# Longer modelled DMA hops for the softmax sums in a statically scheduled kernel

## The chip, the cores and the metric

One core of one Trainium2 chip. The metric is device time in microseconds (us) of one execution. "ScalarE" is ACT in the profile, "VectorE" is DVE, "TensorE" is PE (PEld is its weight load), "GpSimd" is POOL and "SyncE" is SP; SPq is the queue from which SyncE issues DMAs.

## The reference, cut to what matters

The kernel computes two independent heads from inputs of 2048 tokens by 640 features and writes them side by side: a linear state-space recurrence (A), and attention with 32 query heads over one shared key and value head of 20 dimensions (B). The change touches only the softmax of B.

```python
def _B_ref(x, wq, wk, wv, wo):
    B, S, D = x.shape            # 1, 2048, 640
    H = 32
    Dh = D // H                  # 20
    q = (x @ wq).reshape(B, S, H, Dh).transpose(0, 2, 1, 3)
    k = x @ wk
    v = x @ wv
    scores = jnp.einsum("bhqd,bkd->bhqk", q, k) * (Dh ** -0.5)
    p = _softmax(scores, axis=-1)
    o = jnp.einsum("bhqk,bkd->bhqd", p, v)
    return o.transpose(0, 2, 1, 3).reshape(B, S, H * Dh) @ wo
```

## The kernel before

The kernel cuts attention into 32 blocks (4 quarters of the queries times 8 groups of 4 heads), each of 64 score tiles of 128 x 512. TensorE computes a tile into PSUM. Either ScalarE takes its exponential (3 or 2 tiles in one instruction, `PR<-SC`), or VectorE and GpSimd take it by an integer approximation in several passes (`DR<-MB` is the first pass, `DR<-DR` the others; SC and MB name PSUM banks, PR and DR the buffers of the results). TensorE then multiplies the result with the values and sums into one PSUM bank per block (PV). Row 20 of each head's 32 rows holds the softmax sum.

When a block is complete, VectorE evicts the bank to one of two buffers `pvsb`. The sums then go out to DRAM and come back spread over 64 partitions; VectorE takes reciprocals; these go out to DRAM and come back broadcast to all rows; VectorE multiplies (the normalisation, `OT<-pvsb,rdB`). That is four DMA hops for each of 31 blocks. The last block takes another way, through TensorE.

```python
            # in pv(), when a block's last product has been planned
            ev = self.dve(lambda e: e.tensor_copy(p.pvsb[:, slot, :], bank.ap), 620, deps=[op], reads=[bank.key],
                          writes=[f"pvsb{slot}"], prio=self.PVEV,
                          gate=lambda: b < 2 or (b - 2 in self.norm_op and self.s.done([self.norm_op[b - 2]])))
            ...
            self.pv_gate = [ev]          # the next block's PV waits for this eviction: one bank
```

No order of instructions is written down by hand. When the kernel is built, a scheduler plays it through with an assumed duration for every operation, picks at each moment the ready operation with the smallest `prio` for each engine, and so fixes every engine's program order. The emitter then puts semaphore waits where data dependencies need them. After that nothing of the assumed times is left, only the order. A DMA's assumed end is:

```python
        if op.dma_key is not None:                       # in Schedule.begin()
            self.free[eng] = self.t + op.tail * len(op.fns)
            s = max(self.t + 1300.0, self.dma_free.get(eng, 0.0))
            self.dma_free[eng] = s + op.dur
            op.end = max(s + op.dur + 700.0, self.free[eng] + 1700.0) + op.land
```

A transposing load is one operation of five DMAs that nothing in the queue can pass. The row of biases `brow` that each query block needs goes into QT by a DMA on the same queue:

```python
        self.ct_op = [self.loadT([(p.CT[:, ri, cd, :], src[:, 128 * cd:128 * cd + 128]) for cd in range(NC)], 819200,
                                 f"ct{ri}", writes=[f"CT{ri}"]) for ri, src in ((0, self.C_re), (1, self.C_im))]
        ...
        self.row_op[(qb, half)] = self.dma(fns, 32768, f"row{rs}", ...   # QT<-brow
```

## Time and profile before

The three runs before the change were 785.99 to 786.46 us, median 786.22 us. The profiled execution has a span of 782.0 us (its time as a run was 783.7 us, so it was faster than those three).

| reading | value |
|---|---|
| ScalarE busy | 754.3 of 782.0 us (96%) |
| exponentials on ScalarE | 737.4 us for 1625 tiles, 0.454 us a tile |
| tiles on VectorE | 423 of 2048 |
| VectorE busy | 654.7 us (84%) |
| VectorE idle before the 31 reciprocals / 31 normalisations | 0.8 / 1.3 us |

From the profile page of the kernel before: the busy time of each engine (share of the span, instructions), and the chain of waits that ended last, by engine.

```profile
PE 731.7 (94%) x10475; PEld 245.0 (31%) x10475; DVE 654.7 (84%) x1193; ACT 754.3 (96%) x675; POOL 444.7 (57%) x460
...
ACT 66%; PE 25%; DVE 5%; DMA 1%; SPq 1%; issue 1%; POOL 0%; ACTq 0%; DVEq 0%; POOLq 0%
```

The Trainium skill, "Perfetto Trace Analysis", section "Identifying the Most-Contended Engine", takes the engine with the highest occupancy as the one to look at; here that is ScalarE (96%), and the chain of waits agrees (66%). From the groups of instructions of the same page: what is written and read, count, then busy us and mean ns of one, then the idle time just before them and who ended most of it.

```profile
L1068 ACT ACTIVATE PR<-SC 128x1536 bf16<-128x1536 f32 (+1 forms) x650 | 737.4, 1340 | 8.6 <-PE MB L571 5.2
...
L586 DVE TENSOR_SCALAR DR<-MB 128x512 int16<-128x512 f32 x423 | 282.7, 684 | 79.2 <-PE MB L571 74.8
```

The count of `DR<-MB`, 423, is the number of tiles that VectorE got. ScalarE's idle time before exponentials is 8.6 us in the whole run. The groups of VectorE in the kernel before, the two that the change is about:

```profile
L581 DVE TENSOR_TENSOR OT<-pvsb,rdB 128x512 bf16<-128x512 bf16 x31 | 16.8, 541 | 1.3 <-DMA rdB<-recs 1.3
...
L1360 DVE RECIPROCAL rc<-dn 64x32 bf16<-64x32 bf16 x31 | 10.4, 334 | 0.8 <-DMA dn<-sums 0.8
```

So VectorE waited for these hops twice in the run, 2.1 us together. Below, VectorE's stream around block 6, from the timeline of the kernel before (start us, duration us, instruction), with all other instructions left out. Evictions at 190.93, 213.82 and 238.63 us are those of blocks 6, 7 and 8.

```profile
190.93 0.69 DVE L1337 CAST pvsb<-MB 128x512 bf16<-128x512 f32 x1
...
196.68 0.33 DVE L1360 RECIPROCAL rc<-dn 64x32 bf16<-64x32 bf16 x1
...
202.94 1.26 DVE L581 TENSOR_TENSOR OT<-pvsb,rdB 128x512 bf16<-128x512 bf16 x1
...
213.82 0.68 DVE L1337 CAST pvsb<-MB 128x512 bf16<-128x512 f32 x1
...
229.04 0.41 DVE L581 TENSOR_TENSOR OT<-pvsb,rdB 128x512 bf16<-128x512 bf16 x1
...
238.63 0.68 DVE L1337 CAST pvsb<-MB 128x512 bf16<-128x512 f32 x1
```

Block 6 is normalised 11 us after the end of its eviction. Its buffer is needed again at 238.63 us, 34 us after the end of the normalisation.

### The profile page before, as it was taken

What the parts mean: (1) busy time and instruction counts of PE and PEld (TensorE: products, weight loads), DVE (VectorE), ACT (ScalarE), POOL (GpSimd) and SP (SyncE); (2) the same over time, 40 slices, a digit from 0 to 9 for tenths busy, and PEclk for the clock granted to TensorE, in tenths of its full rate; (3) what the DMA queues carried; (4) which work ended last, traced back from release to release, by engine and by line L of the source; (5) the groups of instructions that cost most, each with busy time, mean ns of one, the idle gap of its engine ahead of it and who ended that gap; (6) DMA issues with size and microseconds to landing.
All of it is one profiled execution on the core that took longest, in us unless ns stands there. A gap on an engine that the chain in (4) does not pass through costs nothing.

```text
span 782.0 us, 24237 instructions
## 1 busy us (share of the span) xinstructions
PE 731.7 (94%) x10475; PEld 245.0 (31%) x10475; DVE 654.7 (84%) x1193; ACT 754.3 (96%) x675; POOL 444.7 (57%) x460
## 2 busy tenths in 40 slices
PE   8989998998999999989999999989999999999998
PEld 3322222322233333323233223323222322333333
DVE  5989898999988888888989868987789788856995
ACT  5999999999999999999999999999999999999995
POOL 6066566346555556566654754655773456578661
PEclk9999999999999999999999999999999999999999
DMA  9740200000001000020000000110000000010001
GB/s 213 129 78 9 51 9 8 10 3 9 9 10 24 20 18 24 16 43 17 13 12 18 27 16 17 29 29 17 9 16 9 24 23 15 22 30 23 9 9 36
DMA packets 54186, 21.60 MB, mean 28 GB/s; under 512 B 43464, under 2 KB 54080, under 8 KB 54080
## 3 DMA queue, kind: packets, MB, share of 16 engines
q1 hardware_dynamic: 52072, 19.87, 11.7%
q8 instruction: 83, 1.36, 0.7%
q10 hardware_dynamic: 2008, 0.18, 0.2%
q14 instruction: 23, 0.19, 0.1%
HBM read 7.20 MB, written 5.50 MB: 16 GB/s over the span
## 4 chain that ended last, share of the span: by engine, by line
ACT 66%; PE 25%; DVE 5%; DMA 1%; SPq 1%; issue 1%; POOL 0%; ACTq 0%; DVEq 0%; POOLq 0%
ACT PR L1068 66%; PE MB L571 10%; PE MB L567 8%; PE SC L571 7%; DVE DR L586 1%; DMA vrow<-in_A_Dskip_dram 1%; PE SC L567 1%; SPq L556 1%; DVE QT L918 1%; DMA xaT<-in_A_x_dram 0%; DVE VS L585 0%; DVE xbT L797 0%; DVE WO L720 0%; DVE aq L585 0%; DVE fr L586 0%
## 5 line engine op out<-in xcount | busy, mean ns | idle before, releaser
L1068 ACT ACTIVATE PR<-SC 128x1536 bf16<-128x1536 f32 (+1 forms) x650 | 737.4, 1340 | 8.6 <-PE MB L571 5.2
L581 POOL TENSOR_TENSOR DR<-DR,step 128x512 int32<-128x512 int32 x421 | 430.8, 1046 | 315.0 <-DVE DR L586 114.9
L586 DVE TENSOR_SCALAR DR<-MB 128x512 int16<-128x512 f32 x423 | 282.7, 684 | 79.2 <-PE MB L571 74.8
L571 PE MATMUL SC<-QT,KT 32*128 32x512 bf16 x1625 | 253.9, 384 | 35.4 <-ACT PR L1068 25.6
L571 PE MATMUL MB<-DR,VS 128*32 128x512 bf16 x1692 | 225.8, 385 | 2.5 <-DVE pvsb L1337 1.1
L571 PE MATMUL MB<-PR,VP 128*32 128x512 bf16 x1625 | 225.5, 385 | 0.7 <-DVE pvsb L1337 0.3
L571 PE MATMUL MB<-QT,KT 32*128 32x512 bf16 x423 | 154.1, 384 | 2.7 <-DMA QT<-brow 1.8
L571 PEld LDWEIGHTS SC<-QT,KT 32*128 32x128 bf16 x1625 | 64.4, 91 | 268.6 <-ACT PR L1068 178.7
L586 DVE TENSOR_SCALAR DR<-DR 128x1024 int16<-128x1024 int16 (+1 forms) x222 | 83.5, 425 | 7.8 <-PE MB L571 5.6
L571 PEld LDWEIGHTS MB<-PR,VP 128*32 128x32 bf16 x1625 | 57.0, 94 | 66.4 <-issue 49.3
L571 PEld LDWEIGHTS MB<-DR,VS 128*32 128x32 bf16 x1692 | 55.9, 94 | 65.9 <-issue 35.2
L567 PE MATMUL MB<-xaT,BT 128*32 128x512 bf16 x800 | 57.8, 382 | 1.0 <-DMA xaT<-in_A_x_dram 1.0
L581 DVE TENSOR_TENSOR prod<-MB,Z 128x1024 bf16<-128x1024 f32 x40 | 48.7, 1218 | 7.3 <-PE MB L567 6.6
L571 PE MATMUL MB<-xbT,wqf 128*32 128x512 bf16 x640 | 49.0, 387 | 0.7 <-DVE brow L586 0.5
L571 PEld LDWEIGHTS MB<-QT,KT 32*128 32x128 bf16 x423 | 36.3, 91 | 22.0 <-DVE DR L586 10.4
L571 PE MATMUL MB<-KT,VZ 128*32 128x256 bf16 x796 | 41.6, 275 | 0.0
L567 PE MATMUL MB<-WO,OT 128*32 128x128 bf16 (+1 forms) x928 | 40.8, 292 | 0.0
L1633 DVE TENSOR_TENSOR_SCAN g<-sc,hst,u 128x512 bf16<-128x512 f32 x30 | 40.7, 1364 | 0.0
L581 DVE TENSOR_TENSOR prod<-g,tab 128x1024 bf16<-128x1024 bf16 x40 | 32.7, 819 | 0.0
L567 PE MATMUL MB<-CT,xbT 128*32 128x512 bf16 (+1 forms) x640 | 31.2, 300 | 0.1
L567 PE MATMUL MB<-CT,W 128*32 128x512 bf16 (+1 forms) x640 | 29.4, 300 | 0.5 <-issue 0.5
L1456 DVE CAST stg<-MB 128x512 bf16<-128x512 f32 x35 | 23.9, 684 | 5.9 <-PE MB L567 5.6
(124 smaller groups left out, 386.3 us busy)
## 6 DMA issues: line engine op xcount, KB each, us to landing
out_dram<-stg SPq DMA_DIRECT2D x35, 128.0 KB, 1.7
rdB<-recs SPq DMA_DIRECT2D x124, 32.0 KB, 1.9
CT<-in_B_x_dram SPq DMA_DIRECT2D x2, 640.0 KB, 5.6
WO<-in_B_wo_dram SPq DMA_DIRECT2D x4, 200.0 KB
wqf<-in_B_wq_dram SPq DMA_DIRECT2D x1, 680.0 KB, 5.3
out_dram<-PR SPq DMA_DIRECT2D x5, 128.0 KB, 1.9
sums<-pvsb SPq DMA_DIRECT2D x31, 4.0 KB
dn<-sums SPq DMA_DIRECT2D x31, 4.0 KB, 1.9
```

The costliest lines, as they stand in the source:

```text
L556: fns = [lambda e, o=o, i=i: e.dma_start_transpose(o, i) for o, i in pairs]
L567: r = e.matmul(out[32 * j:32 * j + 32], lhsT=lhsT[:, 32 * j:32 * j + 32], rhs=rhs, start=start, stop=stop, tile_position=(0, 32 * j), skip ...
L571: return lambda e: e.matmul(out, lhsT=lhsT, rhs=rhs, start=start, stop=stop, **kw)
L581: return lambda e: e.tensor_tensor(out, a, b, op)
L586: return lambda e: e.tensor_scalar(out, a, s1, s2, op0=op0, op1=op1)
L918: ev = self.dve(lambda e: e.tensor_copy(dst, bank.ap), 600, deps=[prev], reads=[bank.key], writes=[key], prio=self.EV)
L1068: ex = self.act(lambda e: e.activation(dst, t[:, 0:512 * n], ACT.Exp, scale=1.0 / UNIT), 0.8333 * 512 * n + 64, deps=[op], reads=[b.key fo ...
L1456: ev = self.dve(lambda e: e.tensor_copy(st, bank.ap), 620, deps=[prev], reads=[bank.key], writes=[key], prio=self.EV, gate=(lambda: last.e ...
L1633: o = self.dve(lambda e, ri=ri, init=init: e.tensor_tensor_scan(p.g[:, u, ri, :], rdec, p.u[:, ri, :], init, ALU.mult, ALU.add), 1280, por ...
```

## The change

The intent: a hop that takes longer on the chip than in the schedule makes VectorE, which runs its stream in order, stand still at the reciprocal or the normalisation. If the schedule assumes longer hops, both stand later in the stream, behind other work, and their data have landed by the time VectorE gets to them.

```diff
+    LATE_DMA = 2000.0
+
     def normalize(self, b, ev):
@@ cut: the same argument is added to each of the four hops
-        o = self.dma(lambda e: e.dma_start(sums, p.pvsb[20:117:32, slot, :]), 4096, f"sum{slot}", deps=[ev], reads=[pv],
+        o = self.dma(lambda e: e.dma_start(sums, p.pvsb[20:117:32, slot, :]), 4096, f"sum{slot}", land=self.LATE_DMA, deps=[ev], reads=[pv],
@@ cut: dn (sums back), rc (reciprocals out), rb (reciprocals back, broadcast) likewise
```

## The prediction

> **What bounds the kernel now.** ScalarE. The page gives ACT 754.3 us busy of 782.0 (96%), PE 94%, VectorE 84%, GpSimd 57%. In the table of stretches ACT is busy 97.4 to 99.7 us of every 100 between 100 and 700 us; it idles at the start (11 us before 60 us) and in the tail (10 us after 770 us). The chain of waits that ended last runs 66% through ScalarE's exponentials, 25% through TensorE, 5% through VectorE, 1% through DMA. By the groups of instructions the exponentials take 737.4 us for 1625 score tiles (0.454 us each); the other 423 of 2048 go to VectorE. So time = start + 0.454 us x ScalarE's tiles + few us of stalls + tail.
>
> **What the change does.** No instruction is added or removed. The engines' program order comes from a schedule made at build time. 2000 ns are added to the modelled landing of each of a block's four DMA hops (sums out, sums back, reciprocals out, spread back). So in VectorE's stream the reciprocal comes about 4 us later, the normalisation about 8 us later, 31 times, and what follows from them is planned later.
>
> **What it can win.** VectorE runs in order, so a hop slower than modelled stalls everything behind it. But the groups show hardly any: idle before the 31 reciprocals 0.8 us in total (one case), before the 31 normalisations 1.3 us (one case). By the trace's landing times the reciprocal starts a median 1.1 us after its data land, the normalisation 2.8 us. The hops take 1.9 us (sums back) and 1.7 us (reciprocals out) from issue to landing, the four issues of the spread 3.1 to 4.6 us. The Trainium skill, "DMA: Bandwidth & Descriptors", section "Anatomy of one DMA", gives a fixed cost of about 2.0 us for another issuing path; these hops are close. The real hops are covered already: 2.1 us of idle can vanish on an engine that is not the bound (127 us idle, 79 of it before its first passes over scores, waiting for TensorE). On the critical path: under 1 us.
>
> **What it can cost.** Eviction to normalisation takes 11 to 20 us now, then 19 to 28; an eviction needs the normalisation of two blocks before, whose eviction was some 46 us earlier: no stall. The output projection of a quarter starts up to 8 us later, with nobody waiting. In the tail the normalisation of block 30 (764.8 us now) falls near the last eviction (771.2 us); TensorE is nearly full from 770 to 779 us with other blocks' work: 0 to 0.5 us.
>
> **What is left is reshuffling.** The greedy schedule changes from the first block on, and with it how many tiles VectorE gets (423; the cap of a quarter is not reached): 5 fewer are 2.3 us. I can't tell its sign; in a tuned kernel a random reshuffle more often loses.
>
> **Prediction.** 787.5 us, 8 in 10 between 782 and 795. Faster by over 2%: 0.02; within 2%: 0.93; slower by over 2%: 0.05.
>
> **What would show it.** Right: VectorE's idle before reciprocal and normalisation goes from 2.1 us to about 0; eviction to normalisation some 8 us longer in the timeline; exponentials within 5 us of 737; ACT still 96%; the difference in time is the change of ScalarE's tile count times 0.454 us plus that of its idle time. Wrong: evictions of the PV sums waiting for normalisations, TensorE idle before the output projection, ScalarE idle above 12 us between 60 and 770 us, or a tile count that moved by over 15.
>
> **What would make it wrong.** A later normalisation that holds projections in a bank that score tiles need, or a VectorE tile count that moves by more than 30.

## The result, and the profile after

The kernel after took 785.89 us (median; 784.59 to 787.01, 4 runs), the kernel before on the same chip 786.34 us (785.99 to 787.09, 4 runs). The ratio is 0.9992, 95% interval 0.9975 to 1.001: the same. Ratios in this text are the mean time of one kernel's runs over the mean of the other's runs in the same rounds, so they are not quite the ratio of the medians. Executions over 1.5% slower than the fastest of the same kernel are left out of the means.

The groups of the kernel after (same view and columns as before; line numbers moved by two):

```profile
L1068 ACT ACTIVATE PR<-SC 128x1536 bf16<-128x1536 f32 (+1 forms) x648 | 734.9, 1353 | 13.6 <-PE MB L571 9.6
...
L586 DVE TENSOR_SCALAR DR<-MB 128x512 int16<-128x512 f32 x428 | 285.8, 683 | 80.2 <-PE MB L571 74.9
```

and the two VectorE groups of the kernel after:

```profile
L581 DVE TENSOR_TENSOR OT<-pvsb,rdB 128x512 bf16<-128x512 bf16 x31 | 14.4, 467 | 0.0
...
L1362 DVE RECIPROCAL rc<-dn 64x32 bf16<-64x32 bf16 x31 | 10.3, 333 | 0.2 <-DMA dn<-sums 0.2
```

The second fence shows the intent fulfilled: 2.1 us of waiting became 0.2 us. The first shows what else happened: VectorE got 5 more tiles, so the exponentials take 2.5 us less (737.4 to 734.9), and ScalarE idles 5.0 us more before them (8.6 to 13.6). That sums to +2.5 us, which is the difference of the two profiled spans (784.5 less 782.0). Of the 5.0 us of idle time, 4.9 lie before 65 us of the run (6.1 against 1.2). The profile thus says 2.5 us slower while the medians say 0.45 us faster, and both have to be explained.

How far the two operations moved, worked out from the start times in the timelines and the landing times of the DMAs:

| over 31 blocks | before | after |
|---|---|---|
| eviction's end to reciprocal, median us | 5.0 | 8.9 |
| sums landed to reciprocal, median us | 1.1 | 5.0 |
| eviction's end to normalisation, median (longest) us | 14.2 (19.9) | 23.5 (44.9) |
| reciprocals landed to normalisation, median us | 2.8 | 7.2 |
| normalisation's end to the next eviction of its buffer, median (shortest) us | 30.8 (25.0) | 21.8 (0.25) |

The medians are as intended. The extremes are not: one normalisation came 44.9 us after its eviction. It is that of block 6. From the timeline of the kernel after, VectorE's stream, the same instructions as shown of before:

```profile
199.93 0.68 DVE L1337 CAST pvsb<-MB 128x512 bf16<-128x512 f32 x1
...
209.37 0.33 DVE L1362 RECIPROCAL rc<-dn 64x32 bf16<-64x32 bf16 x1
...
221.58 0.68 DVE L1337 CAST pvsb<-MB 128x512 bf16<-128x512 f32 x1
...
245.53 0.75 DVE L581 TENSOR_TENSOR OT<-pvsb,rdB 128x512 bf16<-128x512 bf16 x2
246.20 0.69 DVE L1337 CAST pvsb<-MB 128x512 bf16<-128x512 f32 x1
```

The normalisations of blocks 6 and 7 stand together (`x2`), and the eviction of block 8 comes directly behind them: it needs block 6's buffer. From ScalarE's timeline of the kernel after, in brackets the idle time before:

```profile
248.69 13.66 ACT L1068 ACTIVATE PR<-SC 128x1024 bf16<-128x1024 f32 x12 [1.96 <-PE MB L571]
```

Two microseconds after that eviction ScalarE had idled 1.96 us, waiting for TensorE's PV products. The kernel before ran through this stretch without a stop:

```profile
224.78 37.65 ACT L1068 ACTIVATE PR<-SC 128x1536 bf16<-128x1536 f32 x33
```

The larger difference between the two profiles lies at the start, before the change has had any effect: the first DMA that it concerns is issued at 55.9 us in before, and up to TensorE's wait at 45 us the two kernels run the same instructions. The table of 5 us stretches has, in each row, busy us (instructions) of PE, PEld, DVE, ACT and POOL, then the granted TensorE clock, DMA share and GB/s. The kernel before:

```profile
45.00:50.00 5.00, 3.22 (x42) 0.97 (x38) 3.09 (x6) 3.81 (x4) 3.46 (x4) 1.00 0.71 64
50.00:55.00 5.00, 4.69 (x73) 1.67 (x71) 4.88 (x11) 5.00 (x5) 2.28 (x3) 1.00 0.49 102
55.00:60.00 5.00, 4.11 (x50) 1.37 (x47) 4.92 (x9) 5.00 (x6) 2.94 (x4) 1.00 0.05 10
```

The kernel after:

```profile
45.00:50.00 5.00, 2.11 (x15) 0.45 (x15) 2.03 (x4) 2.12 (x3) 3.22 (x4) 0.76 0.21 49
50.00:55.00 5.00, 5.00 (x48) 1.03 (x44) 2.90 (x7) 3.24 (x3) 0.00 (x0) 0.50 0.76 122
55.00:60.00 5.00, 5.00 (x51) 1.40 (x54) 2.77 (x6) 4.03 (x4) 2.77 (x3) 0.50 0.00 0
```

The clock fell to half and ScalarE lost time. From the clock records the low clock lasted from 47.6 to 61.3 us. TensorE's timelines show what came before it. The kernel before:

```profile
47.26 0.37 PE L571 MATMUL MB<-QT,KT 32*128 32x512 bf16 x1 [1.76 <-DMA QT<-brow]
```

and the kernel after:

```profile
48.15 0.58 PE L571 MATMUL MB<-QT,KT 32*128 32x512 bf16 x1 [2.89 <-DMA QT<-brow]
```

Both wait for the first bias row; in the profiled run of after it landed 0.9 us later and the clock dropped. All four runs of after have a mean granted clock of 0.989 to 0.993, the profiled run of before 0.998. In the later rounds the kernel before shows both cases: in the last set of 11 runs, the seven at a clock of 0.991 or less took 786.0 to 787.8 us (mean 786.9), the four at 0.997 or more 780.2 to 783.2 us (mean 782.3). So the profile of before shows one of its lucky executions, which explains why the profiles disagree with the medians. This is an inference from the clock of each run; only the profiled runs show where in time the clock was low.

### The profile page after: what moved, and what is told of

Same layout as the page of the kernel before. It is cut to its first block, busy times and chain, and to the rows that moved or that the text cites. A ratio compares the mean times of both kernels' runs of the same rounds, so it can differ in the third digit from the quotient of the medians.

```text
span 784.5 us, 24250 instructions
## 1 busy us (share of the span) xinstructions
PE 732.4 (93%) x10458; PEld 242.7 (31%) x10458; DVE 657.4 (84%) x1205; ACT 751.7 (96%) x673; POOL 453.7 (58%) x471
## 4 chain that ended last, share of the span: by engine, by line
ACT 71%; PE 20%; DVE 6%; DMA 1%; issue 1%; POOL 0%; ACTq 0%; SPq 0%; DVEq 0%; POOLq 0%
ACT PR L1068 71%; PE MB L571 8%; PE SC L571 6%; PE MB L567 6%; DVE DR L586 1%; PE SC L567 1%; DMA vrow<-in_A_Dskip_dram 1%; DVE QT L918 1%; DVE VS L585 0%; DVE xbT L797 0%; DVE prod L581 0%; DVE WO L720 0%; DVE aq L585 0%; DVE pvsb L1337 0%; SPq L964 0%
## 5 line engine op out<-in xcount | busy, mean ns | idle before, releaser
L1068 ACT ACTIVATE PR<-SC 128x1536 bf16<-128x1536 f32 (+1 forms) x648 | 734.9, 1353 | 13.6 <-PE MB L571 9.6
L581 POOL TENSOR_TENSOR DR<-DR,step 128x512 int32<-128x512 int32 x432 | 439.7, 1040 | 309.1 <-DVE DR L586 84.2
L586 DVE TENSOR_SCALAR DR<-MB 128x512 int16<-128x512 f32 x428 | 285.8, 683 | 80.2 <-PE MB L571 74.9
L571 PE MATMUL MB<-PR,VP 128*32 128x512 bf16 x1620 | 221.4, 387 | 0.4 <-DVE pvsb L1337 0.2
L571 PE MATMUL MB<-QT,KT 32*128 32x512 bf16 x428 | 156.6, 388 | 3.6 <-DMA QT<-brow 2.9
L571 PEld LDWEIGHTS MB<-PR,VP 128*32 128x32 bf16 x1620 | 55.3, 94 | 62.3 <-issue 46.4
L571 PE MATMUL MB<-xbT,wqf 128*32 128x512 bf16 x640 | 46.0, 382 | 0.8 <-DVE brow L586 0.5
L567 PE MATMUL MB<-WO,OT 128*32 128x128 bf16 (+1 forms) x928 | 39.2, 292 | 0.2 <-DVE prod L581 0.2
L581 DVE TENSOR_TENSOR prod<-g,tab 128x1024 bf16<-128x1024 bf16 x40 | 35.4, 884 | 0.0
L567 PE MATMUL MB<-CT,xbT 128*32 128x512 bf16 (+1 forms) x640 | 30.8, 301 | 0.1
```

Of the source, the lines that this page charges most:

```text
L567: r = e.matmul(out[32 * j:32 * j + 32], lhsT=lhsT[:, 32 * j:32 * j + 32], rhs=rhs, start=start, stop=stop, tile_position=(0, 32 * j), skip ...
L571: return lambda e: e.matmul(out, lhsT=lhsT, rhs=rhs, start=start, stop=stop, **kw)
L581: return lambda e: e.tensor_tensor(out, a, b, op)
L586: return lambda e: e.tensor_scalar(out, a, s1, s2, op0=op0, op1=op1)
L1068: ex = self.act(lambda e: e.activation(dst, t[:, 0:512 * n], ACT.Exp, scale=1.0 / UNIT), 0.8333 * 512 * n + 64, deps=[op], reads=[b.key fo ...
```

## The experiments

Twelve kernels were run, all correct. They were in three sets (the first four rows, the next four, the last four); those of one set ran on one chip and share the runs of before. A difference between kernels of different sets is a difference of medians, for which no interval was taken. "Idle" of ScalarE is the idle time before exponentials in the groups of the profiled run.

| run | edit | us, median | ratio to before (95% interval) | ScalarE tiles | exponentials, us | ScalarE idle, us |
|---|---|---|---|---|---|---|
| before_row | before, bias row first | 780.43 | 0.9928 (0.9913 to 0.9943) | 1625 | 737.1 | 5.9 |
| after_row | after, bias row first | 781.26 | 0.9937 (0.9921 to 0.9952) | 1620 | 734.3 | 9.0 |
| late_10 | hops +10 ns | 783.79 | 0.9970 (0.9955 to 0.9985) | 1624 | 736.7 | 9.6 |
| late_12000 | hops +12000 ns | 969.2 (all six runs) | 1.2306 (1.2267 to 1.2344) | 1573 | (slow run) | (slow run) |
| before_hop2 | before, two unplanned hops | 885.47 | 1.1245 (1.1201 to 1.1288) | 1625 | 749.1 | 101.4 |
| after_hop2 | after, two unplanned hops | 805.42 | 1.0253 (1.0231 to 1.0276) | 1620 | 736.5 | 28.6 |
| early_1500 | hops -1500 ns | 846.93 | 1.0772 (1.0746 to 1.0799) | 1617 | 741.8 | 69.6 |
| late_8000 | hops +8000 ns | 836.98 | 1.0647 (1.0626 to 1.0667) | 1602 | 728.6 | 67.7 |
| row_norm6 | after_row, block 6's normalisation preferred | 777.72 | 0.9915 (0.9884 to 0.9947) | 1623 | 736.0 | 4.1 |
| row_25 | bias row first, hops +25 ns | 780.11 | 0.9934 (0.9905 to 0.9963) | 1623 | 735.8 | 7.5 |
| row_4000 | bias row first, hops +4000 ns | 784.19 | 0.9987 (0.9958 to 1.0017) | 1623 | 736.1 | 9.6 |
| before_row_norm | before_row, all normalisations preferred | 780.69 | 0.9947 (0.9913 to 0.9980) | 1621 | 735.1 | 8.6 |

The runs of before beside them had medians of 785.77, 785.91 and 786.14 us.

### The start made equal: before_row and after_row

```diff
-                                 f"ct{ri}", writes=[f"CT{ri}"]) for ri, src in ((0, self.C_re), (1, self.C_im))]
+                                 f"ct{ri}", writes=[f"CT{ri}"], gate=lambda: (0, 0) in self.row_op and self.row_op[(0, 0)].start is not None) for ri, src in ((0, self.C_re), (1, self.C_im))]
```

The same edit goes into before and into after. The order of every compute engine stays exactly that of the kernel edited; on the DMA queue the first bias row passes one transposing load.

> The kernel before with one DMA order changed: the transposing loads of C wait until the first bias row (QT<-brow) has been issued. The instruction streams of all compute engines are identical to before. Theory (the start differs by chance of one DMA): the row's data land some 5 us earlier, the 1.8 us (before) or 2.9 us (after) of TensorE idle at 45 us vanish, the granted clock stays 1.00 between 45 and 65 us, mean clock at least 0.997; time 786.3 minus 2 to 6 us. Rival (the dip of the clock at 48 us belongs to the changed order, not to the wait): no change, within 1 us.

> The kernel after with the same one DMA order changed. Theory: the dip of the granted clock to 0.50 at 48 to 62 us vanishes; with equal starts the kernel after then keeps what its 5 fewer ScalarE tiles are worth (5 x 0.454 = 2.3 us): faster than before_row by 1 to 4 us, 777 to 783 us. Rival (later normalisations cost something that cancels the win): equal to before_row within 1 us or slower.

From the timeline of the DMA queue, the issue of the row in before

```profile
43.10 2.96 SPq L964 DMA_DIRECT2D QT<-brow  x4
```

and in before_row

```profile
37.43 2.97 SPq L964 DMA_DIRECT2D QT<-brow  x4
```

The row is issued 5.7 us earlier. before_row took 780.43 us against 785.77 us, and its six runs have a clock of 0.998 to 1.000. The stretch that was shown of before and after reads so in before_row, with ScalarE (the fourth pair after the length) busy all of it and the clock at 1.00:

```profile
45.00:50.00 5.00, 4.82 (x67) 1.62 (x62) 4.79 (x10) 5.00 (x6) 3.04 (x4) 1.00 0.86 111
```

So the theory holds: the dip belonged to the wait, not to the change. Wait and dip together were worth about 5 us in either kernel (785.77 less 780.43 in one set; 785.89 less 781.26 across two sets).

The second expectation was a miss. after_row was to be 1 to 4 us faster than before_row, for its 5 fewer tiles; its median was 0.8 us above, and the runs overlap (779.62 to 781.8 us and 780.45 to 781.8 us), so its gain of tiles had gone. The table says why: exponentials 2.8 us less, ScalarE idle 3.1 us more. In after_row's ScalarE timeline one stop is as long as that:

```profile
242.91 20.45 ACT L1068 ACTIVATE PR<-SC 128x1024 bf16<-128x1024 f32 x18 [3.14 <-PE MB L571]
```

It is the place of the double normalisation again, here in VectorE's timeline of after_row:

```profile
238.57 0.75 DVE L581 TENSOR_TENSOR OT<-pvsb,rdB 128x512 bf16<-128x512 bf16 x2
239.24 0.68 DVE L1337 CAST pvsb<-MB 128x512 bf16<-128x512 f32 x1
```

TensorE had other work meanwhile. Its PV products go on behind the eviction, from TensorE's timeline of after_row:

```profile
240.80 1.84 PE L571 MATMUL MB<-DR,VS 128*32 128x512 bf16 x17
```

(Here the clock records also have a low clock from 238.6 to 242.0 us, which the profiled run of after lacks; there the stop was 1.96 us. So the hold alone showed about 2 us, and with the dip 3.1 us.)

### Was it the normalisation of block 6? row_norm6

```diff
-                                   reads=[pv, rb], writes=[f"OT{ot}"], prio=self.EV, gate=lambda: self.ot_free(b))
+                                   reads=[pv, rb], writes=[f"OT{ot}"], prio=0.4 if b == 6 else self.EV, gate=lambda: self.ot_free(b))
```

> after_row with one operation changed: the normalisation of block 6 gets a higher priority in the build-time scheduler. In after_row two normalisations (blocks 6 and 7) stand together at 238.6 us, 36 us after block 6's reciprocal, and directly before the eviction of block 8, which needs block 6's buffer; ScalarE then idles 3.1 us at 242.9 us. Orders are identical until about 207 us. Theory (a normalisation planned so late that it holds the eviction two blocks on costs ScalarE 3 us, and that is where after's tile gain went): the normalisation of block 6 within 25 us of its reciprocal, the 3.1 us stall near 243 us gone, ScalarE idle before the exponentials 9.0 down to 5 to 7 us; with 1623 tiles the time is 779 to 781.5 us, equal to or below after_row's 781.3 although ScalarE has 3 more tiles (1.4 us). Rival (the stall near 243 us has another cause, as the work of the first projection): the stall stays, idle 9 us, 782.5 us or more.

VectorE's stream in row_norm6, the same view as before:

```profile
193.49 0.68 DVE L1337 CAST pvsb<-MB 128x512 bf16<-128x512 f32 x1
...
202.94 0.34 DVE L1362 RECIPROCAL rc<-dn 64x32 bf16<-64x32 bf16 x1
...
214.26 0.39 DVE L581 TENSOR_TENSOR OT<-pvsb,rdB 128x512 bf16<-128x512 bf16 x1
214.85 0.69 DVE L1337 CAST pvsb<-MB 128x512 bf16<-128x512 f32 x1 [0.20 <-PE MB L571]
...
234.49 0.69 DVE L1337 CAST pvsb<-MB 128x512 bf16<-128x512 f32 x1
...
238.21 0.41 DVE L581 TENSOR_TENSOR OT<-pvsb,rdB 128x512 bf16<-128x512 bf16 x1
```

Block 6 is normalised at 214.26 us, 11 us after its reciprocal. The eviction of block 8 moves from 239.24 to 234.49 us, before block 7's normalisation. ScalarE's timeline has no stop there:

```profile
224.33 30.43 ACT L1068 ACTIVATE PR<-SC 128x1024 bf16<-128x1024 f32 x27
```

The time is 777.72 us, below the expected range; ScalarE's idle time is 4.1 us, also below what was expected. With the eviction no longer held, the stop is gone: the held eviction was its cause. The rest of the gain is not proven to be the same cause: from that normalisation on, at 214 us, the order differs, and the placebos below show what a new order alone can do. Its median is the lowest, 0.9915 of before. Most of that is the bias row's part, since before_row alone has 0.9928. Its six runs are 777.34 to 781.4 us, the slowest of them at a clock of 0.993. Its interval to before_row and after_row was not taken, since they ran in different sets, so it is not shown to be faster than before_row.

### How much does a new order alone move? late_10 and row_25

```diff
-    LATE_DMA = 2000.0
+    LATE_DMA = 10.0
```

and 25.0 with the bias row first.

> A placebo: the modelled hops longer by 10 ns in place of 2000. It removes no wait and moves nothing by intent, but the greedy schedule shuffles: 1624 ScalarE tiles (before 1625, after 1620). Theory (what is left is reshuffling): as far from before as after is, within 4 us either way. Rival (the 2000 ns do something of their own, for good or bad): placebo equal to before within 0.5 us in time, in idle time of ScalarE and in tiles.

> A second placebo, with the mended start: hops modelled 25 ns longer, 1623 ScalarE tiles (before_row 1625). Theory (reshuffling alone moves the time by about what the change moved it): within 2.5 us of before_row's 780.4 us, with idle time of ScalarE before the exponentials between 4 and 9 us and the difference explained by 0.454 us x tiles plus the change of that idle time, to within 1 us. Rival (the order as such makes no difference at all below 2000 ns): within 0.3 us of before_row.

late_10 came out at 783.79 us (0.9970), further from before than the real change is (0.9992). All its five runs have a clock of 0.991 to 0.993, and its profile has the dip at the start (low from 47.5 to 57.8 us, after a wait of 1.96 us), so it is not faster for want of a dip; part of its 9.6 us of idle time is the dip. The seven runs of before at a clock of 0.993 in the same set have a mean of 785.8 us, so the 2 us are not a matter of the clock either. row_25 is 0.3 us from before_row in the median, but its parts moved by more: exponentials 1.3 us less, ScalarE idle 1.6 us more. (In time alone this is as near to the rival, 0.3 us, as to the theory.) So a change of 10 or 25 ns that is meant to do nothing moved the time by up to 2 us, and its parts by 1 to 2 us that may cancel.

### Does the order buy tolerance? before_hop2 and after_hop2

Two more DRAM-to-DRAM copies of the sums, each waiting for the one before, are put in after the schedule is made. The compute engines' orders are exactly those of before and of after.

```diff
+    HOPS = 2
+    def more_hops(self):                      # called between s.run() and the emitter
+        order = []
+        for op in self.s.order:
+            if op.dma_key in ("dn0", "dn1"):
+                ...                           # HOPS copies sums -> bounce -> bounce
+                op.reads = [key]              # dn now reads the last copy
+            order.append(op)
+        self.s.order = order
```

> The kernel before with two more real DRAM-to-DRAM copies of the sums between the first and the second hop, which the schedule does not know of: the streams of all compute engines are identical to before, only the data of the reciprocal come some 4 to 5 us later. Slack before is a median 1.1 us. Theory (an in-order VectorE pays for what the schedule does not cover): VectorE idle before the 31 reciprocals goes from 0.8 us to about 31 x 3.3 = 100 us, and the time rises by 15 to 70 us (over 2%). Rival (the reciprocal's wait is never on the critical path): within 1% of before.

> The same two copies in the kernel after, streams of the compute engines identical to after. Slack after is a median 5.0 us at the reciprocal and 7.2 us at the normalisation. Theory (the change bought tolerance, nothing else): VectorE idle before reciprocals and normalisations below 25 us in total, the time within 1% of after. Rival (a longer real hop costs as much in either order): slower by as much as before_hop2.

VectorE's group of reciprocals in before_hop2

```profile
L1362 DVE RECIPROCAL rc<-dn 64x32 bf16<-64x32 bf16 x31 | 10.7, 345 | 88.6 <-DMA dn<-bounce 88.6
```

and in after_hop2

```profile
L1364 DVE RECIPROCAL rc<-dn 64x32 bf16<-64x32 bf16 x31 | 10.5, 337 | 15.2 <-DMA dn<-bounce 15.0
```

The same longer hop costs before 99.6 us (885.47 less 785.91) and after 19.5 us (805.42 less 785.89). That is what the change bought. Its expectation for the wait (below 25 us) held; that for the time (within 1%) missed, since it was 2.5%. VectorE is not the busiest engine, yet 87.8 us more of its waiting went with 99.6 us more time, and 15.0 us with 19.5 us: a bit over one for one. No other DMA accounts for it: in before_hop2 the normalisations wait 0.0 us for theirs, and TensorE 2.0 us for the bias row (1.8 us in before). The waits view says how it gets there: VectorE's first passes stand behind the waiting reciprocal, and TensorE's score tiles wait for them (in total us, times, longest us). The kernel before, then before_hop2:

```profile
PE SC L571 <- DVE DR L586: 1.9, 7, 0.5
```

and

```profile
PE SC L573 <- DVE DR L588: 34.8, 22, 3.8
```

Part of the cost is the clock: its mean was 0.927 in before_hop2's profile and 0.977 in after_hop2's. How much was not separated.

### The other way: early_1500

```diff
-    LATE_DMA = 2000.0
+    LATE_DMA = -1500.0
```

> The modelled hops 1500 ns shorter than in before: the reciprocal stands 3 us earlier in VectorE's stream, the normalisation 6 us, before their data can have landed (slack 1.1 and 2.8 us). 1617 ScalarE tiles. Theory: real stalls of VectorE, about 2 us before most reciprocals and 1 to 2 us before normalisations, 60 to 120 us idle in total before them; time +5 to +50 us. Rival (order is irrelevant in this range): within 0.5% of before less 3.6 us for 8 fewer tiles.

VectorE's group of reciprocals in early_1500:

```profile
L1362 DVE RECIPROCAL rc<-dn 64x32 bf16<-64x32 bf16 x31 | 10.7, 345 | 60.7 <-DMA dn<-sums 60.7
```

Every one of the 31 reciprocals waits now, 60.7 us in all, and normalisations wait another 9.4 us. The time rose by 61 us (846.93 less 785.91), 11 us more than the range had it. Here too the clock was lower in the profile, 0.962, and its part of the cost was not separated. The cliff on this side is near: before has a median of 1.1 us of slack.

### How late is too late? row_4000, late_8000, late_12000

LATE_DMA was 4000.0 (with the bias row first), 8000.0 and 12000.0.

> Hops modelled 4000 ns longer, with the mended start; 1623 ScalarE tiles. Normalisations then stand 27 to 39 us after the eviction in the schedule, still short of the 46 us at which the next eviction of the same buffer is due, so no eviction is held. Theory (there is a plateau up to the two-block limit, and a steep rise behind it, as 8000 and 12000 showed): 777 to 785 us, ScalarE idle before the exponentials below 12 us. Rival (every us of lateness costs in proportion, 51 us for 8000 ns): near 800 us.

> The modelled hops longer by 8000 ns; 446 VectorE tiles, 1602 for ScalarE. Theory (order alone counts): no idle before reciprocal and normalisation, exponentials 1602 x 0.454 = 727 us, time 772 to 788 us. Rival (modelled waits turn into real ones): slower than before by over 2%.

> The modelled hops longer by 12000 ns: in the build-time schedule evictions now wait for the normalisations of two blocks before, ScalarE's fills stall there and VectorE gets more tiles: 475 in place of 423, so 1573 for ScalarE. Theory (after the build only the order counts; the real hops are as short as ever, no engine waits for a DMA): idle before reciprocal and normalisation about 0, exponentials 1573 x 0.454 = 714 us; VectorE and GpSimd get 52 x 0.87 = 45 us more, so ScalarE's idle time grows; 765 to 790 us. Rival (a modelled wait of 48 us more per block is a real one): over 850 us.

late_8000 and late_12000 refute the theory that went with them, that a wait which exists only in the schedule cannot cost anything. No VectorE instruction waits for a hop in late_8000; still it takes 836.98 us with 23 fewer ScalarE tiles than before. Its group of exponentials:

```profile
L1068 ACT ACTIVATE PR<-SC 128x1536 bf16<-128x1536 f32 (+1 forms) x641 | 728.6, 1321 | 67.7 <-PE MB L571 63.2 <-PE SC L571 4.3
```

The longest of the stops, in VectorE's timeline of late_8000:

```profile
430.59 0.41 DVE L581 TENSOR_TENSOR OT<-pvsb,rdB 128x512 bf16<-128x512 bf16 x1
...
431.99 0.68 DVE L1337 CAST pvsb<-MB 128x512 bf16<-128x512 f32 x1
```

In TensorE's timeline of late_8000, waiting for that eviction:

```profile
432.72 1.47 PE L571 MATMUL MB<-DR,VS 128*32 128x512 bf16 x12 [3.17 <-DVE pvsb L1337]
```

And in ScalarE's timeline of late_8000:

```profile
435.52 27.37 ACT L1068 ACTIVATE PR<-SC 128x1536 bf16<-128x1536 f32 x24 [6.42 <-PE MB L571]
```

Each eviction stands right behind the normalisation that frees its buffer (median 0.7 us between them over the run, 30.8 us in before), and that stands behind other work which the schedule put into the wait. TensorE waits for the eviction, its one PV bank being full, and ScalarE waits for TensorE to free the exponentials' buffers. (In the stop shown the clock records also have a low clock from 432.1 to 435.5 us; over the run the mean clock was 0.959, and how much of the 51 us it cost was not separated.) The other stops look alike, though TensorE mostly had other work while the PV products were held: of ScalarE's 21 stops of over 1 us before exponentials, 19 ended with a PV product, 1.2 to 4.5 us after the end of an eviction. The modelled wait has become real as order.

row_4000 has no eviction that close: the shortest distance is 5.5 us. It takes 784.19 us, within the expected range, but 3.8 us above before_row, with 3.7 us more ScalarE idle. So the plateau is not flat; whether these 3.8 us are due to lateness or to one more shuffle, one run of that size cannot tell.

late_12000 took 961.57 to 977.9 us; its profiled run was slow, so no line of it is used.

### A candidate: before_row_norm

```diff
-                                   reads=[pv, rb], writes=[f"OT{ot}"], prio=self.EV, gate=lambda: self.ot_free(b))
+                                   reads=[pv, rb], writes=[f"OT{ot}"], prio=0.4, gate=lambda: self.ot_free(b))
```

> Candidate for a version that beats both: the kernel before, the mended start, and every normalisation given a higher priority in the scheduler (0.4 in place of 0.52), without longer modelled hops; 1621 ScalarE tiles against 1625. Theory (tiles x 0.454 us plus idle): 777 to 781 us, about 1.8 us below before_row if ScalarE's idle time stays near 6 us. Rival (priority of the normalisation displaces first passes over scores and ScalarE waits more): above 781 us.

It took 780.69 us, inside the range, but not below before_row: exponentials 2.0 us less, ScalarE idle 2.7 us more. Preferring every normalisation gained nothing where none was late. It also ate into the margin: two normalisations now wait for their reciprocals, 3.5 us in all (1.2 us in before_row).

## Why the prediction was right or wrong

The forecast of the time was right: 787.5 us was predicted, 782 to 795, and 785.89 us was measured; the two kernels are the same within 2%.

Right in its parts:

- VectorE's waits for the hops went from 2.1 to 0.2 us, as "to about 0" had it, and the medians moved by 3.9 and 9.3 us (4 and 8 predicted).
- The exponentials stayed within 5 us of 737 (734.9). The difference of the two profiles is the change of the exponentials (-2.5 us) plus that of ScalarE's idle time (+5.0 us), the bookkeeping that the prediction named.
- "What is left is reshuffling": a placebo of 10 ns moved the time by 2 us, more than the change did (0.45 us in the medians).

Wrong, or right by luck:

- "Eviction to normalisation ... then 19 to 28; ... no stall" failed: seven of the 31 normalisations came later than 28 us, one of them at a price. The longest is 44.9 us. The prediction had itself named "evictions of the PV sums waiting for normalisations" as a sign that it was wrong; that sign did appear, once. The step that failed is adding 8 us to the old distances: the added delay only sets when a normalisation becomes *ready*; when it is *picked* depends on what else VectorE has at that time. Block 6's became ready and was passed over for so long that the eviction of block 8 had to wait for its buffer. It cost 2 to 3 us of ScalarE's time, about what 5 fewer tiles had gained; that the two cancelled is luck. row_norm6 showed it. Why it was passed over was read from the scheduler, which was run again on the kernel after: in its own time block 6's normalisation is ready at 207.2 us and placed at 233.2 us, behind 37 other VectorE operations, of which 19 are first passes over scores that it prefers (`prio` 0.50 against 0.52). For most of that time its rule that a normalisation must not overlap certain GpSimd operations (`port=True`) also held it back. The eviction of block 8 is ready at 227.1 us there and placed at 233.9 us.
- "2.1 us of idle can vanish on an engine that is not the bound ... under 1 us" used a wrong principle. With unplanned hops, VectorE's waits went with about as much time, or somewhat more, though VectorE is busy only 84%. It runs in order, and the waits view shows TensorE's score tiles waiting for the first passes behind it. What these two waits (0.8 and 1.3 us) were worth was not measured.
- The prediction did not see the start. The wait for the bias row and the drop of the clock at 48 us are worth 5 us in both kernels, more than anything that the change did.

## What to carry to other kernels

In a statically scheduled kernel an assumed latency is a margin: too short and every use becomes a real wait (here 61 us for 1.5 us less per hop), too long and a buffer is freed so late that the order itself makes the wait (51 us for 8 us more per hop), and between them (up to 2 us more here; 4 us more is unclear) a change of it mostly reshuffles. Look for the extremes, not the medians, of such a distance, above all for the shortest one between a buffer's last reader and its next writer. And before explaining 2 us between two profiles, look at the granted clock over the first stretch, where both kernels run the same instructions.

## What the Trainium skill lacked or had wrong

- "TensorE: Matmul & The Clock Gate", section "HAM oscillation — how this bites in real kernels", warns of TensorE idle gaps over about 3.4 us. Here a wait of 1.96 us (late_10) and one of 2.89 us (after) were followed by half clock; 1.76 us (before) was not. The page's section "Part 1: The HAM clock gate (the "warmup" mystery)" gives a free-running window of 3413 ns; the low periods of these profiles, 3.4, 6.8, 10.2 and 13.7 us long where the end of the run does not cut them, agree with multiples of that. In after_row the clock fell for 3.4 us at 238.6 us, and the longest gap of TensorE in the 10 us before was 0.95 us; what lowered it there was not tested.
- No page that was read says what the drop costs a kernel that ScalarE bounds: 4.6 us here, by the two groups of before's runs (786.9 and 782.3 us).
- "DMA: Bandwidth & Descriptors", section "Anatomy of one DMA — SWDGE (gpsimd) path", has about 2.0 us of fixed cost for DMAs issued by GpSimd. The hops here are issued by SyncE; with 4 KB they took a median 1.9 us (sums back) and 1.7 us (reciprocals out), so the figure comes close for this path too. The page has no such figure for a DMA that waits behind others in its queue: the bias row was issued 5.7 us later for standing behind one transposing load of five DMAs.
- "Perfetto Trace Analysis", section "Identifying the Most-Contended Engine", goes by occupancy. An engine that is busy 84%, next to one of 96%, still cost about 1 us of time for each us that it had to wait (87.8 us of waits, 99.6 us of time, part of it by the lower clock).
